# Splitting the 576 tokens of a unit into two halves of 288 in the token mixing of an attention-mixer kernel

## Chip, core and metric

The kernel runs on one core of one Trainium2 chip. The metric is device time in microseconds (us) of one execution, taken as the median of several runs of the same kernel.

## What is computed

For 8 batches and 8 heads, with 576 tokens and 64 channels per head, the reference does linear attention and then a two-stage mixer, all in float32:

```
q_s = softmax(q, over the 64 channels);  k_s = softmax(k, over the 576 tokens)
kv  = k_s^T v                 per head, 64 x 64
x   = q_s kv                  heads side by side: 576 tokens x 512 channels per batch
h   = relu(x^T w_tok1) w_tok2        576 -> 256 -> 576, mixes tokens
u   = x + h^T
out = u + relu(u w_ch1) w_ch2        512 -> 1536 -> 512, mixes channels
```

## The kernel before

**Units and groups.** A unit is a pair of heads of one batch, so it covers 128 channels and 576 tokens. There are 32 units (NU), four per batch. The rows of a unit are stored as five chunks of 128: four chunks hold the tokens 0 to 511, and the fifth holds the last 64 tokens (TL) twice. The eight batches of 576 tokens stand in one row of 4608 token columns, cut into nine groups (NG) of 512 columns. A batch therefore ends inside a group, at column `edge` of the batch, and every unit writes to two groups. The arrays `uT[g]` hold a group's u, split into a high and a low part ("uh" and "ul"), in which the matmuls of the channel mixing read it.

**Channel mixing.** It takes most of the time and is written out as a list of steps: `ch1(g, f)` (12 matmuls of 512 columns, line 488), its ReLU by ACT (L491) and the low part by DVE (L492), and one step later `ch2` (12 matmuls of 512 columns, L648). The last two groups are done in another way (lines 618 to 641, matmuls L597). The work of the units is put between these steps by hand (`put(at, ...)`, lines 803 to 842), and a scheduler of the framework that goes by a time simulation orders instructions where the program leaves it open.

**Early units.** The first 8 units (batches 0 and 1, "early") run before the channel mixing starts. The token weights are loaded and converted to float32 by DVE and ACT in the same stretch. `stage_qT` turns q with TensorE and copies it out (L341, L344). `stage_y` and `stage_h1` are matmuls L375 and L383. `stage_u` makes u in two pieces: a float32 matmul with `kvf` (L428, recorded as two passes) and six matmuls with the second token weight (`token_products`, L412), all of 320 columns in the first piece and of 256 in the second.

**Late units.** The other 24 units run `stage_us`. Here the 576 token columns are taken by the half of a 128-row chunk in which they lie ("side" 0 or 1): side 0 has five runs of 64 tokens, 320 columns, and side 1 has four, 256 columns. The token weights are read in those runs with a step (`cols`, lines 443 to 446). After the 12 `token_products` (six per side, L412) come four float32 matmuls of 64 x 64 (L458), one for each side and head; each is recorded as two passes. They lie on the four quarters of the array: the side gives the rows, the head gives the columns. Their moving operand is `stack`, which `stage_qT` fills from a DVE transpose (L352) in 16 pieces of 32 rows, 11 by DVE and 5 by ACT (L362). Then `empty` moves each bank to uh (ACT, L416) and ul (DVE, L417), in two pieces per side where the group's edge falls within the side; it writes every other run of 64 columns. Only the columns of one step stand in the code:

```
w = u["kvf"][rows, hs] if side == h else u["kvo"][rows]
to = t[hs, 0 : n * D].rearrange("p (c t) -> p c t", t=D)
nc.tensor.matmul(to, w, u["stack"][rows, h, 0:n, :], start=False, stop=True)
```

**The last 64 tokens twice.** In late units `softmax_q` splits q into a high part qh (ACT, L117) and a low part ql (POOL, L118). In the fifth chunk, rows 64 to 127 of qh are replaced by those of ql (L300, ACT, 64 rows), so that two matmuls do there what takes three in the other chunks. In early units the second copy is kept out by zeros in the upper half of `w1f` (L210, L214), and in k^T v by zeros in v and in its column of ones (L60).

**Loads.** `load_v` brings v in three transfers on SP's queue: two of the four whole chunks (L172, one per head, runs of 256 bytes) and one of 64 rows of the fifth (L173). The first loads go out in this order: kt and q of unit 0, three pieces of weights, v of unit 0, kt and q of unit 1, v of unit 1. One memory of eight banks serves all matmul results; two banks are held by a late unit's two sides.

Of the kernel before, what the change touches and what calls it, by code (L numbers as in the profile page):

```python
# [20 lines left out]
def attn_mixer_kernel(ctx: ExitStack, tc: tile.TileContext, q, k, kt, v, wt, out, dims):  # L21
# [9 lines left out]
    C1 = C + 1  # L31
    S0 = C * P
    TL = S - S0
    NG = B * S // CW
    NU = B * NJ
    NE = 2 * NJ
# [20 lines left out]

    def v_places(t):
        nc.gpsimd.memset(t[:, :, :, D : D + 1], 1.0)
        nc.gpsimd.memset(t[TL:P, C, :, :], 0.0)  # L60
        return t

    v_ring = [v_tile(const)]
# [2 lines left out]
    nc.gpsimd.memset(ones, 1.0)  # L66


    ebias = const.tile([P, 1], F32, name="ebias")
    nc.gpsimd.memset(ebias, -(896.0 + 20.0) * 2.0**23)  # L70

# [34 lines left out]
            cw[f] = [t[:, f - f0, :, x, :] for x in range(4)]  # L106

    ch_rows(0, F_HEAD)

    Q = 32  # L110

    def f32(ap):
        return ap.bitcast(F32)
# [54 lines left out]
    def load_v(n):  # L168
        if n < NU and n not in v_of:
            t = v_ring[n % 2 if n < NE or n >= PAIRED else 0]  # L170
            for h in range(2):
                nc.sync.dma_start(t[:, 0:C, h, 0:D], v[n][:, 0:C, h * D : (h + 1) * D])  # L172
            nc.sync.dma_start(t[0:TL, C, :, 0:D], v[n][0:TL, C, :].rearrange("p (h d) -> p h d", h=2))  # L173
            v_of[n] = t

    def load_weights(i, n=CW, out=None):
# [30 lines left out]
    def load_tok1():  # L207

        flat = w1f.rearrange("p c t -> p (c t)")
        nc.gpsimd.memset(w1f[TL:P, C, :], 0.0)  # L210
        for i in range(N1):
            load_weights(AT_T1 + i, out=flat[:, i * CW : (i + 1) * CW])
        load_weights(AT_TAIL, TOK, out=w1t)
        nc.scalar.copy(w1f[0:TL, C, :], w1t[0:TL])  # L214

    def split_tok1():
        split(w1h, w1l, w1f[:, 0:C, :], nc.vector)
# [55 lines left out]
    def softmax_q(u):  # L273
        G = 2 * C1
        st = sm.tile([P, 3, G], F32, name="st")
        qc = u["q"]
        qt = qc.rearrange("p c (h d) -> p (c h) d", h=2)
        nc.vector.tensor_reduce(st[:, 0, :], qt, axis=AX.X, op=ALU.max)
        if u["n"] < NJ or NE <= u["n"] < NE + NJ:

            nc.vector.tensor_scalar(st[:, 0, :], st[:, 0, :], -1.0, None, op0=ALU.mult)
            for i in range(G):
                one = slice(i, i + 1)
                nc.scalar.activation(
                    qt[:, i, :], qt[:, i, :], AF.Exp, bias=st[:, 0, one], accum_out=st[:, 1, one]
                )
# [12 lines left out]

        nc.scalar.copy(qh[TL:P, C, :], f32(ql[TL:P, C, :]))  # L300
        u["qh"], u["ql"] = qh, ql

    def stage_kv(u):
# [29 lines left out]
    def stage_qT(u):  # L333

        qx = u["q"]
        if u["early"]:
            qt = early.tile([P, S], F32, name="qt")
            t = ps_unit()
            for c in range(C):
                nc.tensor.transpose(t[:, c * P : (c + 1) * P], qx[:, c, :], f32(ident))  # L340
            nc.scalar.copy(qt[:, 0:S0], t)  # L341
            t = ps_unit()
            nc.tensor.transpose(t[:, 0:P], qx[:, C, :], f32(ident))
            nc.scalar.copy(qt[:, S0:S], t[:, 0:TL])  # L344
            u["qt"] = qt
            return

        stack = wk.tile([P, 2, S], F32, name="stack")[:, :, 0 : C1 * D]
        u["stack"] = stack = stack.rearrange("p h (c t) -> p h c t", t=D)

        turned = cv.tile([P, C1 * P], U32, name="cv_s").bitcast(F32).rearrange("p (c t) -> p c t", t=P)
        nc.vector.transpose(turned, qx)  # L352
        k = 0
        for x in range(P // Q):
            side, at = divmod(x * Q, D)
            for y in range(P // Q):
                h, row = divmod(y * Q, D)
                row += side * D
                eng = (nc.vector.tensor_copy, nc.vector.tensor_copy, nc.scalar.copy)[k % 3]
                k += 1  # L360
                n = C1 - side
                eng(stack[row : row + Q, h, 0:n, at : at + Q], turned[x * Q : (x + 1) * Q, 0:n, y * Q : (y + 1) * Q])  # L362

    def stage_y(u):
# [32 lines left out]

    emptied = []

    def token_products(u, t, N, cols, start, stop):  # L400
        mm = []
        for n in range(NT):
            mm += [
                (u["hh"][:, n, :], cols(w2h, n)),
                (u["hh"][:, n, :], cols(w2l, n)),
                (u["hl"][:, n, :], cols(w2h, n)),
            ]
        for i, (a, w) in enumerate(mm):
            to = t[:, 0:N]
            if len(w.shape) == 3:  # L410
                to = to.rearrange("p (c t) -> p c t", t=D)
            nc.tensor.matmul(to, a, w, start=start and i == 0, stop=stop and i == len(mm) - 1)  # L412

    def empty(uh, ul, src):
        emptied[:] = [
            nc.scalar.copy(uh, src).ins,  # L416
            nc.vector.tensor_tensor(ul, src, f32(uh), op=ALU.subtract).ins,  # L417
        ]

    def stage_u(u, half):  # L420
        b, j = u["b"], u["j"]
        edge = (b + 1) * CW - b * S
        cut = min(max(edge, S - 320), 320)
        n0, n1 = ((0, cut), (cut, S))[half]
        N = n1 - n0
        ns = slice(n0, n1)
        t = ps_unit()
        nc.tensor.matmul(t[:, 0:N], u["kvf"], u["qt"][:, ns], start=True, stop=False)  # L428
        token_products(u, t, N, lambda w, n: w[:, n, ns], False, True)
        for g, a0, a1 in ((b, n0, min(n1, edge)), (b + 1, max(n0, edge), n1)):  # L430
            if a0 < a1:
                at = b * S + a0 - g * CW
                uh, ul = (x[:, j, at : at + a1 - a0] for x in uT[g])
                empty(uh, ul, t[:, a0 - n0 : a1 - n0])

    def stage_us(u):
        b, j = u["b"], u["j"]
        edge = (b + 1) * CW - b * S  # L440
# [18 lines left out]
        for side, t in enumerate(banks):  # L459
            n = C1 - side  # L460
            src = t[:, 0 : n * D].rearrange("p (c t) -> p c t", t=D)
            m = len([c for c in range(n) if c * P + side * D < edge])
            for g, c0, c1 in ((b, 0, m), (b + 1, m, n)):
                if c0 < c1:
                    at = (b * S + c0 * P + side * D - g * CW) // D
                    uh, ul = (
                        x[:, j, :].rearrange("p (c t) -> p c t", t=D)[:, at : at + 2 * (c1 - c0) - 1 : 2, :] for x in uT[g]
                    )
                    empty(uh, ul, src[:, c0:c1, :])


    drained = []
# [434 lines left out]
    out_end(NG - 1, acc, True)  # L907


def pieces(w_tok1, w_tok2, w_ch1, w_ch2):  # L910

    import numpy as np

    S, TOK = w_tok1.shape
    C, TL, NT = S // P, S % P, TOK // P
# [3 lines left out]
    tail[0, :, :TOK] = np.concatenate([w_tok1[C * P :]] * 2)  # L919
# [44 lines left out]
```

## Time and profile before

| | |
|---|---|
| median of 3 runs | 797.1 us (796.87 to 797.65) |
| profiled execution | 798.31 us, of it a span of 796.5 us from its first to its last instruction |
| TensorE busy | 781.0 us of the span, 4478 matmul records |
| DVE, ACT, POOL busy | 526.9, 331.9 and 83.4 us |
| mean granted TensorE clock | 0.994 of full speed |
| moved by DMA | 65.10 MB, 64276 packets |

The profile is a recording of one execution on the chip. PE is TensorE (matmuls), PEld its weight loads, DVE is VectorE, ACT is ScalarE, POOL is GpSimd; SPq is SyncE's queue that issues transfers. L458 is line 458 of the kernel. A matmul's recorded duration reaches into the next one, since matmuls are pipelined, so the time that one costs is read from start to start. Of an f32 matmul the two passes are recorded one by one.

### The profile page before, as it was taken

Reading aid. Unit: us, or ns where it says so; the run is one execution under the profiler, and the core shown is the slowest. Engines: PE = TensorE matmul, PEld = TensorE weight load, DVE = VectorE, ACT = ScalarE, POOL = GpSimd, SP = SyncE. Lnnn points to the kernel's source line nnn. Section 1 sums busy time; section 2 is a strip of 40 time slices with the busy share of each in tenths; the row PEclk is TensorE's granted clock in tenths of the full one; section 3 lists DMA queues with packets and bytes.
Section 4 is the critical chain, followed back from the end, with each engine's and each line's share of the span. In section 5 each row is a group of like instructions: output and inputs, shape, how many; then the busy total and the mean of one; then the engine's idle time right before and its main releaser. Section 6 shows DMA issues by size and latency. Waiting matters only on the chain.

```text
span 796.5 us, 12193 instructions
## 1 busy us (share of the span) xinstructions
PE 781.0 (98%) x4478; PEld 651.9 (82%) x4478; DVE 526.9 (66%) x1224; ACT 331.9 (42%) x896; POOL 83.4 (10%) x72
## 2 busy tenths in 40 slices
PE   6899999999999999999999999999999999999997
PEld 5688888888888788888888888888888888888886
DVE  6889999876776445655575555563767458975440
ACT  6977554455643343243433434343434413332100
POOL 1000010011112111020200201111111000000020
PEclk8899999999999999999999999999999999999999
DMA  9754333324334221513132222212240000000011
GB/s 289 236 160 132 105 126 107 107 78 128 87 102 136 65 75 35 152 36 99 39 106 67 80 57 80 92 54 81 51 126 18 1 1 32 22 1 0 1 67 40
DMA packets 64276, 65.10 MB, mean 82 GB/s; under 512 B 41432, under 2 KB 44760, under 8 KB 64216
## 3 DMA queue, kind: packets, MB, share of 16 engines
q1 hardware_dynamic: 59608, 56.06, 23.9%
q10 hardware_dynamic: 4608, 8.26, 2.7%
q8 instruction: 35, 0.57, 0.3%
q14 instruction: 25, 0.20, 0.1%
HBM read 54.85 MB, written 9.45 MB: 81 GB/s over the span
## 4 chain that ended last, share of the span: by engine, by line
PE 94%; DVE 2%; DMA 1%; SPq 1%; ACT 1%; issue 0%; DVEq 0%
PE ps_o L648 33%; PE ps_h L488 29%; PE ps_h L597 7%; PE ps_h L375 6%; PE ps_h L412 6%; PE ps_h L648 4%; PE ps_h L310 2%; PE ps_h L458 2%; PE ps_h L383 2%; DMA kt_t<-in_kt 1%; PE ps_o L375 1%; PE ps_o L412 1%; PE ps_o L428 0%; DVE mc L241 0%; PE ps_h L428 0%; DVE stg L197 0%
## 5 line engine op out<-in xcount | busy, mean ns | idle before, releaser
L648 PE MATMUL ps_o<-h2h,cw 128*128 128x512 f32 x768 | 225.5, 391 | 0.0
L488 PE MATMUL ps_h<-uh,cw 128*128 128x512 f32 x672 | 210.1, 393 | 0.0
L648 PEld LDWEIGHTS ps_o<-h2h,cw 128*128 128x128 f32 x768 | 142.5, 188 | 29.8 <-DVE stg L685 0.5
L492 DVE SCALAR_TENSOR_TENSOR h2l<-ps_h,h2h 128x512 fp32r<-128x512 f32 x84 | 57.8, 689 | 152.6 <-ACT h2h L491 152.6
L488 PEld LDWEIGHTS ps_h<-uh,cw 128*128 128x128 f32 x672 | 123.7, 188 | 24.5 <-issue 0.5
L648 PE MATMUL ps_o<-h2l,cw 128*128 128x512 f32 x384 | 137.3, 391 | 0.0
L488 PE MATMUL ps_h<-ul,cw 128*128 128x512 f32 x336 | 131.0, 390 | 0.0
L648 PEld LDWEIGHTS ps_o<-h2l,cw 128*128 128x128 f32 x384 | 71.9, 188 | 15.3 <-DVE h2l L492 0.3
L118 POOL TENSOR_TENSOR ql<-q_t,qh 128x640 fp32r<-128x640 f32 x24 | 38.2, 1590 | 421.2 <-ACT qh L117 383.6
L491 ACT ACTIVATE h2h<-ps_h 128x512 fp32r<-128x512 f32 x84 | 50.0, 595 | 71.9 <-PE ps_h L488 70.8
L488 PEld LDWEIGHTS ps_h<-ul,cw 128*128 128x128 f32 x336 | 63.1, 188 | 13.4
L362 DVE COPY stack<-cv_s 32x160 f32<-32x160 f32 (+1 forms) x264 | 56.2, 231 | 3.6 <-PE ps_h L458 0.7
L270 POOL TENSOR_TENSOR k_t<-k_t,mb 128x640 f32<-128x640 f32 x24 | 38.2, 1590 | 119.4 <-DMA mb<-row 83.3
L271 ACT ACTIVATE k_t<-k_t 128x640 f32<-128x640 f32 x24 | 17.8, 741 | 72.1 <-POOL k_t L270 70.7
L506 DVE TENSOR_TENSOR ul<-ps_h,ul 128x512 f32<-128x512 f32 x40 | 27.5, 692 | 24.2 <-PE ps_h L597 23.9
L416 ACT CAST uh<-ps_h 128x128 fp32r<-128x128 f32 (+4 forms) x104 | 27.6, 288 | 30.7 <-PE ps_h L458 20.2
L362 ACT COPY stack<-cv_s 32x128 f32<-32x128 f32 (+1 forms) x120 | 36.9, 308 | 2.8 <-DVE cv_s L352 1.5
L417 DVE TENSOR_TENSOR ul<-ps_h,uh 128x128 fp32r<-128x128 f32 (+4 forms) x104 | 30.8, 312 | 6.0 <-ACT uh L416 5.1
L412 PE MATMUL ps_h<-w2h,hh 128*128 128x320 f32 (+1 forms) x112 | 33.7, 302 | 0.0
L412 PE MATMUL ps_h<-w2l,hh 128*128 128x320 f32 (+1 forms) x112 | 33.1, 298 | 0.0
L648 PE MATMUL ps_h<-cw 128*128 128x512 f32 x144 | 33.0, 389 | 0.0
L412 PE MATMUL ps_h<-w2h,hl 128*128 128x320 f32 (+1 forms) x112 | 32.6, 298 | 0.2 <-DVE hl L391 0.2
(249 smaller groups left out, 1283.8 us busy)
## 6 DMA issues: line engine op xcount, KB each, us to landing
stg<-in_w SPq DMA_DIRECT2D x28, 512.0 KB, 4.2
kt_t<-in_kt SPq DMA_DIRECT2D x32, 320.0 KB, 2.9
q_t<-in_q SPq DMA_DIRECT2D x32, 320.0 KB, 3.4
k_t<-in_k SPq DMA_DIRECT2D x24, 320.0 KB
out<-stg ACTq DMA_DIRECT2D x27, 256.0 KB, 2.0
v_t<-in_v SPq DMA_DIRECT2D x46, 128.0 KB, 2.7
part<-in_v SPq DMA_DIRECT2D x18, 128.0 KB, 2.5
mb<-row SPq DMA_DIRECT2D x23, 64.0 KB, 3.0
```

The lines of the kernel that those rows point to most:

```text
L118: return lo_eng.tensor_tensor(lo, src, f32(hi), op=ALU.subtract).ins
L270: nc.gpsimd.tensor_tensor(kx, kx, mb.unsqueeze(1).broadcast_to([P, C1, P]), op=ALU.subtract)
L362: eng(stack[row : row + Q, h, 0:n, at : at + Q], turned[x * Q : (x + 1) * Q, 0:n, y * Q : (y + 1) * Q])
L375: nc.tensor.matmul(y[:, 0:TOK], a, w, start=(i == 0), stop=(i == len(mm) - 1))
L412: nc.tensor.matmul(to, a, w, start=start and i == 0, stop=stop and i == len(mm) - 1)
L416: nc.scalar.copy(uh, src).ins,
L417: nc.vector.tensor_tensor(ul, src, f32(uh), op=ALU.subtract).ins,
L488: nc.tensor.matmul(t, cw[f][x][:, n, :], w, start=(i == 0), stop=(i == 3 * NJ - 1))
L491: nc.scalar.activation(hh, t, AF.Relu).ins,
L492: nc.vector.scalar_tensor_tensor(hl, t, 0.0, f32(hh), op0=ALU.max, op1=ALU.subtract).ins,
L597: nc.tensor.matmul(t, x(n), w[n], start=(n == 0 and i == 0), stop=(n == 1 and i == 2))
L648: nc.tensor.matmul(to, cw[f][x][:, n0 + n, :], w, start=(first and i == 0), stop=(last and i == 2))
```

## The change

The last 64 tokens (Q is now 32) are divided between the two halves of the rows: rows 0 to 31 of the fifth chunk hold tokens 512 to 543, rows 32 to 63 hold them again, rows 64 to 95 hold tokens 544 to 575 and rows 96 to 127 hold those again. Each half of the rows then has 4 x 64 + 32 = 288 tokens, and the token columns are ordered by halves, in the second token weight, in `uT` and in the output (the host puts the output's columns back and is not timed). `stage_u` and `stage_us` both work on two contiguous pieces of 288 columns; a batch's edge falls into one of the two pieces only. The rows of the second copy ("twins") are two blocks of 32. v comes in two transfers of five chunks, with its zeros from the host. The core of the diff (the host's reordering of weights and inputs is left out):

```diff
+    Q = TL // 2
+    W = S // 2
+    twins = [slice(x, x + Q) for x in (Q, 3 * Q)]
...
         nc.gpsimd.memset(t[:, :, :, D : D + 1], 1.0)
-        nc.gpsimd.memset(t[TL:P, C, :, :], 0.0)
+        for x in twins:
+            nc.gpsimd.memset(t[x, C, :, D : D + 1], 0.0)
...
+    once = const.tile([P, 1], F32, name="once")
+    nc.gpsimd.memset(once, 1.0)
+    for x in twins:
+        nc.gpsimd.memset(once[x], 0.0)
...
             for h in range(2):
-                nc.sync.dma_start(t[:, 0:C, h, 0:D], v[n][:, 0:C, h * D : (h + 1) * D])
-            nc.sync.dma_start(t[0:TL, C, :, 0:D], v[n][0:TL, C, :].rearrange("p (h d) -> p h d", h=2))
+                nc.sync.dma_start(t[:, :, h, 0:D], v[n][:, :, h * D : (h + 1) * D])
...
-        nc.scalar.copy(w1f[0:TL, C, :], w1t[0:TL])
+        nc.scalar.activation(w1f[:, C, :], w1t, AF.Copy, scale=once)
...
-        nc.scalar.copy(qh[TL:P, C, :], f32(ql[TL:P, C, :]))
+        for x in twins:
+            nc.scalar.copy(qh[x, C, :], f32(ql[x, C, :]))
...
-            nc.scalar.copy(qt[:, 0:S0], t)
+            sides = qt.rearrange("p (s x) -> p s x", s=2)
+            chunks = t.rearrange("p (c s t) -> p s c t", c=C, s=2)
+            nc.scalar.copy(sides[:, :, 0 : S0 // 2].rearrange("p s (c t) -> p s c t", c=C), chunks)
...
-            nc.scalar.copy(qt[:, S0:S], t[:, 0:TL])
+            nc.scalar.copy(sides[:, :, S0 // 2 :], t[:, 0:P].rearrange("p (s t) -> p s t", s=2)[:, :, 0:Q])
...
-        stack = wk.tile([P, 2, S], F32, name="stack")[:, :, 0 : C1 * D]
-        u["stack"] = stack = stack.rearrange("p h (c t) -> p h c t", t=D)
+        stack = wk.tile([P, 2, S], F32, name="stack")
+        u["stack"] = stack[:, :, 0:W]
+        stack = stack[:, :, 0 : C1 * D].rearrange("p h (c t) -> p h c t", t=D)
...
-                n = C1 - side
+                n = C1 if at == 0 else C
...
-    def token_products(u, t, N, cols, start, stop):
+    def token_products(u, t, half, start, stop):
+        ns = slice(half * W, (half + 1) * W)
         mm = []
         for n in range(NT):
             mm += [
-                (u["hh"][:, n, :], cols(w2h, n)),
-                (u["hh"][:, n, :], cols(w2l, n)),
-                (u["hl"][:, n, :], cols(w2h, n)),
+                (u["hh"][:, n, :], w2h[:, n, ns]),
+                (u["hh"][:, n, :], w2l[:, n, ns]),
+                (u["hl"][:, n, :], w2h[:, n, ns]),
             ]
         for i, (a, w) in enumerate(mm):
-            to = t[:, 0:N]
-            if len(w.shape) == 3:
-                to = to.rearrange("p (c t) -> p c t", t=D)
-            nc.tensor.matmul(to, a, w, start=start and i == 0, stop=stop and i == len(mm) - 1)
...
+            nc.tensor.matmul(t[:, 0:W], a, w, start=start and i == 0, stop=stop and i == len(mm) - 1)
+
+    def empty(u, t, half):
...
-        cut = min(max(edge, S - 320), 320)
-        n0, n1 = ((0, cut), (cut, S))[half]
-        N = n1 - n0
-        ns = slice(n0, n1)
-        t = ps_unit()
-        nc.tensor.matmul(t[:, 0:N], u["kvf"], u["qt"][:, ns], start=True, stop=False)
-        token_products(u, t, N, lambda w, n: w[:, n, ns], False, True)
...
+    def stage_u(u, half):
+        t = ps_unit()
+        nc.tensor.matmul(t[:, 0:W], u["kvf"], u["qt"][:, half * W : (half + 1) * W], start=True, stop=False)
+        token_products(u, t, half, False, True)
+        empty(u, t, half)
...
     def stage_us(u):
...
         banks = []
-        for side in range(2):
-            def cols(w, n):
-                t = w[:, n, side * D :]
-                t = w[:, n, :].rearrange("p (x t) -> p x t", t=D)
-                return t[:, side : 2 * C + 1 : 2, :]
...
+        for half in range(2):
             t = ps_unit()
-            token_products(u, t, (C1 - side) * D, cols, True, False)
+            token_products(u, t, half, True, False)
             banks.append(t)
-        for side, t in enumerate(banks):
-            rows = slice(side * D, (side + 1) * D)
-            n = C1 - side
+        for half, t in enumerate(banks):
+            rows = slice(half * D, (half + 1) * D)
             for h in range(2):
                 hs = slice(h * D, (h + 1) * D)
-                w = u["kvf"][rows, hs] if side == h else u["kvo"][rows]
-                to = t[hs, 0 : n * D].rearrange("p (c t) -> p c t", t=D)
-                nc.tensor.matmul(to, w, u["stack"][rows, h, 0:n, :], start=False, stop=True)
...
+                w = u["kvf"][rows, hs] if half == h else u["kvo"][rows]
+                nc.tensor.matmul(t[hs, 0:W], w, u["stack"][rows, h, :], start=False, stop=True)
+        for half, t in enumerate(banks):
+            empty(u, t, half)
```

## Rows read from the trace of the kernel before

**Rows 1.** The page, busy time of the engines and the chain that ended last.

```profile
PE 781.0 (98%) x4478; PEld 651.9 (82%) x4478; DVE 526.9 (66%) x1224; ACT 331.9 (42%) x896; POOL 83.4 (10%) x72
...
PE 94%; DVE 2%; DMA 1%; SPq 1%; ACT 1%; issue 0%; DVEq 0%
```

**Rows 2.** Busy time by stretches: us, busy of each engine, PEclk, DMA share, GB/s.

```profile
10.00:20.00 10.00, 5.32 (x37) 4.18 (x37) 9.20 (x23) 6.67 (x26) 0.00 (x0) 0.76 1.07 335
20.00:30.00 10.00, 7.43 (x51) 5.29 (x50) 9.21 (x26) 9.96 (x38) 0.00 (x0) 0.90 0.83 258
30.00:40.00 10.00, 9.05 (x61) 7.96 (x62) 8.75 (x24) 8.93 (x35) 0.00 (x0) 0.83 0.64 217
400.00:660.00 260.00, 260.00 (x1571) 217.38 (x1570) 158.66 (x400) 101.47 (x265) 32.62 (x21) 1.00 0.21 62
```

**Rows 3.** TensorE in order of time, one late unit: start, us, line, shape.

```profile
401.08 0.31 PE L412 MATMUL ps_h<-w2h,hh 128*128 128x320 f32 x1
...
401.97 0.28 PE L412 MATMUL ps_h<-w2h,hh 128*128 128x256 f32 x1
...
402.77 0.48 PE L458 MATMUL ps_h<-stack,part 64*64 64x320 f32 x1
402.78 0.48 PE L458 MATMUL ps_h<-stack,kvo 64*64 64x320 f32 x2
...
403.05 0.38 PE L458 MATMUL ps_h<-stack,kvo 64*64 64x256 f32 x1
...
403.10 0.43 PE L458 MATMUL ps_h<-stack,kvo 64*64 64x320 f32 x1
403.46 0.80 PE L310 MATMUL ps_h<-v_t,k_t 128*64 128x65 f32 x20
```

**Rows 4.** Groups by form, the 64 x 64 matmuls with `kvo`: busy us, mean ns.

```profile
L458 PE MATMUL ps_h<-stack,kvo 64*64 64x320 f32 x48 | 18.0, 454 | 0.0
...
L458 PE MATMUL ps_h<-stack,kvo 64*64 64x256 f32 x48 | 15.4, 402 | 0.0
```

**Rows 5.** The chain of waits in the early units, four pieces: start, us, what.

```profile
69.17 0.54 PE ps_o L428 x2
...
70.15 0.43 PE ps_h L428 x2
...
75.17 0.59 PE ps_o L412 x4
75.76 0.47 PE ps_h L412 x4
```

**Rows 6.** Groups by form, ACT: busy us, mean ns | idle before, releaser.

```profile
L320 ACT ACTIVATE kvf<-ps_h,rs 64x64 f32<-64x64 f32 x34 | 10.6, 311 | 29.3 <-DVE rs L316 28.9
...
L416 ACT CAST uh<-ps_h 128x128 fp32r<-128x128 f32 x36 | 9.2, 266 | 13.2 <-PE ps_h L458 7.3 <-DVE ul L417 5.8
...
L300 ACT CAST qh<-ql 64x128 fp32r<-64x128 f32 x24 | 7.2, 298 | 33.5 <-POOL ql L118 23.7 <-DVE stg L685 9.7
...
L416 ACT CAST uh<-ps_h 128x64 fp32r<-128x64 f32 x22 | 4.5, 216 | 12.5 <-PE ps_h L458 10.8 <-DVE ul L417 1.4
```

**Rows 7.** TensorE's waits: us in total, times, longest.

```profile
PE ps_h L375 <- ACT w1f L214: 0.9, 1, 0.9
```

**Rows 8.** SP's queue in the head, in order of time: start, us.

```profile
3.06 1.93 SPq L172 DMA_DIRECT2D v_t<-in_v  x2
...
5.03 1.53 SPq L173 DMA_DIRECT2D v_t<-in_v  x1
```

**Rows 9.** The chain of waits in the head, the second kt.

```profile
6.61 5.86 DMA kt_t<-in_kt
```

**Rows 10.** Busy time by stretches in the head, columns as in Rows 2.

```profile
4.00:5.00 1.00, 0.99 (x5) 0.69 (x4) 0.97 (x3) 0.18 (x1) 0.00 (x0) 1.00 0.71 187
5.00:6.00 1.00, 0.30 (x3) 0.30 (x4) 0.68 (x2) 0.90 (x2) 0.00 (x0) 1.00 0.89 242
6.00:7.00 1.00, 1.00 (x12) 1.00 (x11) 0.00 (x0) 1.00 (x7) 0.00 (x0) 1.00 0.76 311
```

More of the change, by code (lines that the diff above doesn't have):

```diff
@@ L108, in attn_mixer_kernel @@
     ch_rows(0, F_HEAD)
-    Q = 32
     def f32(ap):
@@ L209, in load_tok1 @@
         flat = w1f.rearrange("p c t -> p (c t)")
-        nc.gpsimd.memset(w1f[TL:P, C, :], 0.0)
         for i in range(N1):
@@ L403, in token_products @@
             mm += [
-                (u["hh"][:, n, :], cols(w2h, n)),
-                (u["hh"][:, n, :], cols(w2l, n)),
-                (u["hl"][:, n, :], cols(w2h, n)),
+                (u["hh"][:, n, :], w2h[:, n, ns]),
+                (u["hh"][:, n, :], w2l[:, n, ns]),
+                (u["hl"][:, n, :], w2h[:, n, ns]),
             ]
         for i, (a, w) in enumerate(mm):
-            to = t[:, 0:N]
-            if len(w.shape) == 3:
-                to = to.rearrange("p (c t) -> p c t", t=D)
-            nc.tensor.matmul(to, a, w, start=start and i == 0, stop=stop and i == len(mm) - 1)
[L414 to L420, printed above, removed]
+            nc.tensor.matmul(t[:, 0:W], a, w, start=start and i == 0, stop=stop and i == len(mm) - 1)
+    def empty(u, t, half):
         b, j = u["b"], u["j"]
         edge = (b + 1) * CW - b * S
-        cut = min(max(edge, S - 320), 320)
-        n0, n1 = ((0, cut), (cut, S))[half]
-        N = n1 - n0
-        ns = slice(n0, n1)
-        t = ps_unit()
-        nc.tensor.matmul(t[:, 0:N], u["kvf"], u["qt"][:, ns], start=True, stop=False)
-        token_products(u, t, N, lambda w, n: w[:, n, ns], False, True)
+        n0, n1 = half * W, (half + 1) * W
         for g, a0, a1 in ((b, n0, min(n1, edge)), (b + 1, max(n0, edge), n1)):
@@ L433, in stage_u @@
                 uh, ul = (x[:, j, at : at + a1 - a0] for x in uT[g])
-                empty(uh, ul, t[:, a0 - n0 : a1 - n0])
+                src = t[:, a0 - n0 : a1 - n0]
+                emptied[:] = [
+                    nc.scalar.copy(uh, src).ins,
+                    nc.vector.tensor_tensor(ul, src, f32(uh), op=ALU.subtract).ins,
+                ]
+    def stage_u(u, half):
[3 more added lines that the diff above has]
+        empty(u, t, half)
@@ L438, in stage_us @@
     def stage_us(u):
-        b, j = u["b"], u["j"]
-        edge = (b + 1) * CW - b * S
         banks = []
-        for side in range(2):
-            def cols(w, n):
-                t = w[:, n, side * D :]
-                t = w[:, n, :].rearrange("p (x t) -> p x t", t=D)
-                return t[:, side : 2 * C + 1 : 2, :]
+        for half in range(2):
             t = ps_unit()
-            token_products(u, t, (C1 - side) * D, cols, True, False)
+            token_products(u, t, half, True, False)
@@ L459, in stage_us @@
[L459 to L469, printed above, removed]
+                w = u["kvf"][rows, hs] if half == h else u["kvo"][rows]
@@ L907, in attn_mixer_kernel, with rows_and_columns @@
     out_end(NG - 1, acc, True)
+def rows_and_columns(S):
+    import numpy as np
+    C, TL = S // P, S % P
+    Q = TL // 2
+    whole, tail = np.arange(C * P).reshape(C, 2, P // 2), np.arange(C * P, S).reshape(2, Q)
+    rows = np.concatenate([whole.ravel(), np.repeat(tail[:, None], 2, axis=1).ravel()])
+    columns = np.concatenate([np.concatenate([whole[:, x].ravel(), tail[x]]) for x in range(2)])
+    return rows, columns
 def pieces(w_tok1, w_tok2, w_ch1, w_ch2):
@@ L914, in pieces @@
     S, TOK = w_tok1.shape
+    w_tok2 = w_tok2[:, rows_and_columns(S)[1]]
     C, TL, NT = S // P, S % P, TOK // P
@@ L918, in pieces @@
     tail = np.zeros((2, P, CW), w_tok1.dtype)
-    tail[0, :, :TOK] = np.concatenate([w_tok1[C * P :]] * 2)
+    tail[0, :, :TOK] = w_tok1[rows_and_columns(S)[0][C * P :]]
     tail[1, :, : NT * TL] = w_tok2[:, C * P :].reshape(NT, P, TL).transpose(1, 0, 2).reshape(P, NT * TL)
@@ L935 @@
     c, tl, nu = s // P, s % P, b * h // 2
-    twice = np.concatenate([np.arange(s), np.arange(s - tl, s)])
+    twice, columns = rows_and_columns(s)
+    once = np.ones((P, c + 1, 1), inputs["v"].dtype)
+    once[:, c].reshape(4, -1)[1::2] = 0
     def rows(x):
@@ L947 @@
         "in_kt": np.ascontiguousarray(inputs["k"].reshape(nu, 2, s, d)[:, :, twice].transpose(0, 1, 3, 2)).reshape(nu, P, -1),
-        "in_v": rows(inputs["v"]),
+        "in_v": np.where(once > 0, rows(inputs["v"]), np.float32(0)),
         "in_w": np.ascontiguousarray(pieces(*weights)),
@@ L962 @@
     o = r.results[0]["out_0"]
-    return np.ascontiguousarray(o.transpose(0, 3, 1, 2)).reshape(b, s, dm)
+    o = o.transpose(0, 3, 1, 2).reshape(b, s, dm)
+    return np.ascontiguousarray(o[:, np.argsort(columns)])
```

## The prediction

> **What bounds the kernel now.** The page comes first: TensorE is busy for 781.0 of 796.5 us, and 94% of the chain that ended last is TensorE's own work [rows 1]. So nearly every microsecond that TensorE's stream of instructions loses or gains is one of the kernel. The stretches say where this does not hold. From 400 to 660 us TensorE is busy for 260.00 of 260 us, while ACT has 101.47 us of work and DVE 158.66 [rows 2]; there only TensorE's own cost counts. From 10 to 30 us TensorE does 5.32 and 7.43 us of work in each 10, DMA is full in the first of the two (share 1.07) and ACT in the second (9.96 of 10), and the granted clock averages 0.76, 0.90 and then 0.83 in the 10 us after [rows 2]; there loads, conversion and clock set the pace. So I read two things in detail: the token stage of one late unit in order of time, and the first 13 us.
>
> **The four quarters of the array, the main term.** In a late unit the 12 `token_products` start at 401.08, the four float32 matmuls of 64 x 64 at 402.77, and the next instruction, of the full height of the array, at 403.46 [rows 3]. The block takes 0.69 us. Its first passes all start within 0.02 us (402.77 and 402.78), so the four quarters work at the same time. Side 1 (256 columns) starts a second pass at 403.05, side 0 (320 columns) its last at 403.10 [rows 3]: each quarter goes at its own pace, the longer side ends the block, and the shorter one's quarters stand idle at its end. With 288 columns on either side the longest pass has 32 columns fewer. The price of a column is in the groups by form: a pass of 320 columns takes 454 ns, one of 256 takes 402 [rows 4]; 52 ns for 64 columns, so 26 ns a pass and 52 ns for the two of a quarter. The group has 48 records of each size, two passes for each of 24 units [rows 4]: 24 x 52 ns = **-1.25 us**.
>
> The bounds are these. If the whole block scaled with its columns, 0.69 x 32/320 = 0.069 us, or -1.65 us. If four quarters at once are slower than two, the pace to take is that of the first pass of side 1, which had all four at work: 256 columns from 402.78 to 403.05, 1.05 ns a column. Side 1 then ends near 403.32 (402.78 and twice 0.27); the longer side would need 402.78 + 640 x 0.81 = 403.30 at the slope's pace and at this one 403.45, so the rows allow either. With four at 1.05 ns a column and two at 0.81, the block now is 512 columns in 0.54 us and the last 128 in 0.10, and after the change 576 in 0.605: -0.036 us a block, or -0.9 us. I take the slope, since it compares the two lengths directly.
>
> The Trainium skill's page "TensorE: Matmul & The Clock Gate" (part 3, measured speedup) speaks for the smaller end: four row tiles at once gave 3.07 times, not four times, the speed of one, so that quarters which now run alone at the end of a block would lose their advantage. By an estimate from that page, with the pace of four a quarter below that of one, the gain would be about 0.9 us. The start times above hold no such slowdown for certain, so the rule stays a bound.
>
> **Token products, nothing.** The columns stay 576 per product, cut otherwise. Six of 320 columns take 401.08 to 401.97, 0.148 us each; six of 256 take until 402.77, 0.80 us with the change to the quarters in it [rows 3]. In the early units, where the operand is contiguous, 320 columns take 0.59/4 = 0.148 and 256 take 0.47/4 = 0.118 us [rows 5]: the runs of 64 of the late units cost nothing now, so contiguous ones bring nothing. A linear price puts 288 at 0.133, twice that is 0.266, the old sum. If 288 cost as much as 256 or as 320 it would be 0.03 us less or more for each of the 6 x 32 pairs, but no row shows a step. The early f32 product follows the same line: 0.54 and 0.43 us for two passes of 320 and 256 columns [rows 5], twice 0.485 after.
>
> **ACT and DVE, hidden.** A late unit's u is emptied in four pieces before (three in batch 7) and in three after: 92 pieces become 72, on both engines, with the same columns. On ACT, 64 columns take 216 ns and 128 take 266 [rows 6], so a piece costs 166 ns beside its columns, and 20 fewer save 3.3 us on ACT and about as much on DVE. Against that, L300 (298 ns, [rows 6]) becomes two copies of 32 rows; rows of a tile work side by side, so I count each at the full 298: 24 x 0.298 = 7.2 us more on ACT. Its cover is the idle time of ACT, 158 us of the 260 after 400 us [rows 2]. The pieces of `stack` keep their number and columns; two of the 160 wide ones only go to other engines. The first half of an early unit now also waits for the copy of the fifth chunk (L344), which stands right behind L341 on ACT and well ahead of the product. The added memsets lie on an idle POOL in the first microseconds. None of this is on TensorE's path; if the cover is gone, see the rivals.
>
> **The tail of w1f, at most 0.1 us.** L214 becomes a copy with a scale of each row, over 128 rows. TensorE waits 0.9 us for it once [rows 7], so it is on the path. A scaled copy of 64 columns takes 311 ns (L320), a plain one 216 [rows 6]: +0.1 us at most, 0 at least; I take **+0.05**.
>
> **Loads of v in the head.** In the head SP issues v of unit 0 as two transfers in 1.93 us from 3.06 and a third in 1.53 us from 5.03 [rows 8], and only then, at 6.61, the second kt; DVE and all that follows wait for that load, 5.86 us [rows 9]. After, the third issue is gone, so kt leaves up to 1.5 us earlier. That helps only as far as the DMA engines had nothing to do: their share was 0.71, 0.89 and 0.76 from 4 to 7 us [rows 10], against 1.07 when full [rows 2], 0.85 us of work missing at most. The other way, v grows from 288 to 320 KB: 32 KB at 187 GB/s [rows 10] is 0.17 us a unit and 0.35 for the two v loads of the head. Between -0.85 and +0.35 I take **-0.1**, nearer the upper end, because an issue that takes 1.5 us is one that is held up by a queue with work in it. Late loads are asked for a unit ahead with a DMA share of 0.21 [rows 2] and cost nothing.
>
> **The sum.** -1.25 + 0.05 - 0.1 = -1.3 us. The profiled execution took 798.31 us, of which 1.8 lie outside its span, and would take 797.0; it stands 1.2 us above the median, so the median goes from 797.1 to **795.8 us**. Its own range, from the bounds, is -1.65 - 0.85 = 794.6 to -0.9 + 0.1 + 0.35 = 796.7.
>
> **Rivals.** *The block does not shrink.* If the quarters share a feed, the total of columns sets the block, which stays the same, and only the small terms are left: 797.1. For it speaks that the pace of the first pass (1.05 ns a column) is above the slope's 0.81; against it, that the shorter side runs ahead.
>
> *The clock gives back more.* A granted clock of 0.83 over the 10 us from 30 [rows 2] is 3.4 us at 1.2 GHz, the rest at 2.4; before it, from 20 to 30 us, TensorE had stood idle for 2.6 us. If an earlier kt closes that gap enough to keep the clock up, 1.7 us of TensorE's work come back: 797.1 - 1.3 - 1.7 = 794.1. The same stretch can come once more in the head, if the larger v makes the gap longer: 797.1 - 1.3 + 1.7 + 0.35 = 797.9.
>
> *Slower.* The second copy of L300 stands on ACT ahead of the next ReLU (L491), whose result TensorE wants one step later. If that ReLU were late, 0.3 us would be lost per unit, 24 x 0.298 - 1.3 = +5.9: 803.0. It decides where ACT reaches the ReLU after its matmuls have ended by more than the step that covers it, 12 matmuls of 512 columns. L300 already waits for POOL, 23.7 us in all [rows 6], without a wait of TensorE's; that speaks against it.
>
> **How the numbers follow.** About 0.2%, 1.6 us, is what a measurement of this kernel can tell from no change, so the line to faster lies at 795.5, just below the forecast. Chances: forecast 0.55, no shrinking 0.16, clock gained 0.17, clock lost 0.06, slower 0.06. Faster is the clock's 0.17 and about a third of the forecast's 0.55, 0.37 in all; slower is 0.06; the same is the rest, 0.57. The range takes in the forecast's own, the unchanged block and the edge of the gained clock: 794.2 to 797.6.
>
> **What would show it.** Right: both passes of the 64 x 64 matmuls near 428 ns, the block at 0.63 to 0.64 us in each of 24 units, the products at 0.133 us, 72 late pieces, no new wait of TensorE. Wrong: a block of 0.69 us; products at another price than 0.133; a wait for h2h or qh on TensorE; another length of the stretches at the lower clock in the first 40 us, which alone could outweigh the main term.

## The result: 805.56 us, slower where no change was forecast

The changed kernel takes 805.56 us in the median of 6 runs, the kernel before 797.19: a ratio of 1.0107 [1.0097, 1.0118]. The forecast was 795.8 within 794.2 to 797.6, and the 8.4 us that came instead belong to none of its rivals. The profiled execution has a span of 803.3 us against 796.5.

The page after, busy time and the chain that ended last, and TensorE's group by form for the 64 x 64 matmuls with `kvo`:

```profile
PE 779.0 (97%) x4478; PEld 651.0 (81%) x4478; DVE 523.5 (65%) x1204; ACT 338.0 (42%) x900; POOL 84.1 (10%) x77
...
PE 80%; DVE 9%; DMA 5%; ACT 3%; issue 1%; POOL 1%; SPq 1%; DVEq 0%; ACTq 0%; POOLq 0%
```

```profile
L454 PE MATMUL ps_h<-stack,kvo 64*64 64x288 f32 x96 | 16.9, 428 | 0.0
```

TensorE is busy for 2.0 us less than before [rows 1], and each pass takes the 428 ns that were forecast. But the chain, 94% TensorE before [rows 1], is 80% now, and DVE, DMA and ACT have 17% of it. (These shares are not the loss: from a single wait the chain runs back over tens of microseconds of the other engines' work.) So the question is not what TensorE does, but what it waits for. Its waits after (engine, line and releaser; us in total, times, longest):

```profile
PE ps_h L317 <- ACT k_t L277: 4.3, 1, 4.3
...
PE ps_h L317 <- DVE h2l L479: 1.9, 1, 1.9
...
PE ps_h L385 <- ACT w1f L220: 1.1, 1, 1.1
PE ps_o L635 <- ACT h2h L478: 1.0, 1, 1.0
```

The 4.3 us and the 1.0 us have no line in the list of before; the wait for h2l was 0.64 us there. TensorE in order of time shows where the largest stands and what follows it (start, us, what, idle before):

```profile
186.84 0.39 PE L635 MATMUL ps_o<-h2l,cw 128*128 128x512 f32 x1
191.56 1.12 PE L317 MATMUL ps_h<-v_t,k_t 128*64 128x65 f32 x20 [4.33 <-ACT k_t L277]
192.61 0.58 PE L385 MATMUL ps_h<-w1h,qh 128*128 128x256 f32 x1
192.99 0.41 PE L385 MATMUL ps_h<-w1l,qh 128*128 128x256 f32 x1
193.21 0.41 PE L385 MATMUL ps_h<-w1h,ql 128*128 128x256 f32 x1
...
195.32 0.29 PE L385 MATMUL ps_h<-w1th,qh 128*128 128x256 f32 x1
195.44 0.28 PE L385 MATMUL ps_h<-w1tl,qh 128*128 128x256 f32 x1
```

After the idle 4.33 us the matmuls of 256 columns start 0.21 us apart (192.99 to 193.21), where the last two stand 0.12 apart. The stretch beside it says why (columns as in rows 2):

```profile
192.00:195.00 3.00, 3.00 (x25) 2.88 (x22) 1.84 (x6) 2.37 (x13) 0.00 (x0) 0.50 0.24 55
```

The granted clock is 0.50 from 192 to 195 us, that is 1.2 GHz in place of 2.4; half of 3 us, 1.5 us, is lost on top of the wait. So 1.00 + 4.33 + 1.5 and the 1.2 us by which the wait for h2l grew (it ends at 282 us; why it grew was not followed) make 8.0 us. Up to 150 us nothing is lost: the same step of `ch1` starts there in both, first before, then after:

```profile
150.42 0.62 PE L488 MATMUL ps_h<-uh,cw 128*128 128x512 f32 x2
```

```profile
150.27 0.61 PE L475 MATMUL ps_h<-uh,cw 128*128 128x512 f32 x2
```

The seventh late unit's 64 x 64 block starts 7.9 us later than before (303.17 against 295.28); from there on 1.1 us is gained, which leaves the 6.8 us between the spans. (The profiled execution before stood 1.2 us above its median.)

**What made k_t late.** The chain of waits, followed back from 191.56 us (start, us, what):

```profile
149.19 4.48 DMA stg<-in_w
...
158.84 3.26 DMA stg<-in_w
...
166.78 0.69 DVE cw L126
167.47 0.75 DVE cv_s L362
...
175.91 2.44 ACT q_t L290 x14
...
178.55 0.59 DVE stg L671
...
181.94 0.60 DVE stg L672
182.53 0.73 DVE q_t L299
...
184.60 0.72 DVE st L284
...
187.37 0.77 ACT q_t L290 x4
...
190.88 0.63 ACT k_t L277
...
191.56 1.12 PE ps_h L317 x20
```

In the kernel before the same view, from 149.91 to 192 us, holds TensorE's rows alone, matmul after matmul. Here it starts at the load of a channel weight (in_w), goes through VectorE's conversion of it (L199 to L206, the last low part by L126 at 166.78), the token work queued behind it, and then through the output of group 1 (`out_end`, L671 and L672), which stands ahead of the normalisation of q of unit 9 ("q norm", L299). Before, the q norm came first and `out_end` after it:

```profile
173.97 0.82 DVE L293 TENSOR_TENSOR q_t<-q_t,st 128x640 f32<-128x640 f32 x1
...
176.38 2.47 DVE L684 TENSOR_TENSOR stg<-ps_o,uh 128x512 f32<-128x512 f32 x4
```

VectorE in order of time, the low parts of the last weight tiles (last columns: shape, count), first in the kernel before, then after:

```profile
133.59 0.68 DVE L118 TENSOR_TENSOR cw<-cv_s,cw 128x512 fp32r<-128x512 f32 x1
135.72 0.68 DVE L118 TENSOR_TENSOR cw<-cv_s,cw 128x512 fp32r<-128x512 f32 x1
141.06 0.69 DVE L118 TENSOR_TENSOR cw<-cv_s,cw 128x512 fp32r<-128x512 f32 x1
...
162.32 0.69 DVE L118 TENSOR_TENSOR cw<-cv_s,cw 128x512 fp32r<-128x512 f32 x1
```

```profile
130.19 1.46 DVE L126 TENSOR_TENSOR cw<-cv_s,cw 128x512 fp32r<-128x512 f32 x2
140.20 1.46 DVE L126 TENSOR_TENSOR cw<-cv_s,cw 128x512 fp32r<-128x512 f32 x2
...
159.50 1.29 DVE L126 TENSOR_TENSOR cw<-cv_s,cw 128x512 fp32r<-128x512 f32 x2
166.78 0.69 DVE L126 TENSOR_TENSOR cw<-cv_s,cw 128x512 fp32r<-128x512 f32 x1 [0.69 <-ACT cw L125]
```

Before, a tile ends every few microseconds; after, two end close together and then none for some 8 us. The program's order of VectorE's instructions says the same; a to e are the five steps of a conversion (L192 to L199 before, L199 to L206 after), the number is the tile, L the low part:

```
before  a24 L b24 c24 d24 a25 e24 b25 c25 L d25 e25 a26 L b26 c26 a27 d26
after   a23 a24 b23 c23 b24 d23 c24 e23 d24 e24 L L a25 b25 a26 c25 b26
```

For these tiles only two staging tiles are there (`more_pools` is closed at F_MORE). Taken in step, both come free together, both loads start together, and VectorE has nothing to convert until they land. Its waits for these loads, in the whole run, first before, then after:

```profile
DVE cv_s L192 <- DMA stg<-in_w: 6.2, 7, 2.5
```

```profile
DVE cv_s L199 <- DMA stg<-in_w: 9.6, 7, 2.9
```

From the first to the last of the last eight low parts it is 28.7 us before (133.59 to 162.32) and 35.8 after (the second of the pair at 130.19 starts at 130.97, the last at 166.78).

So the theory is that the order of VectorE's instructions, which the scheduler chose anew, costs the 8 us, and not the halves themselves.

### The profile page after: what moved, and what is told of

Same layout as the page of the kernel before. It is cut to its first block, busy times and chain, and to the rows that moved or that the text cites. A ratio compares the mean times of both kernels' runs of the same rounds, so it can differ in the third digit from the quotient of the medians.

```text
span 803.3 us, 12112 instructions
## 1 busy us (share of the span) xinstructions
PE 779.0 (97%) x4478; PEld 651.0 (81%) x4478; DVE 523.5 (65%) x1204; ACT 338.0 (42%) x900; POOL 84.1 (10%) x77
## 4 chain that ended last, share of the span: by engine, by line
PE 80%; DVE 9%; DMA 5%; ACT 3%; issue 1%; POOL 1%; SPq 1%; DVEq 0%; ACTq 0%; POOLq 0%
PE ps_o L635 27%; PE ps_h L475 23%; PE ps_h L584 7%; PE ps_h L385 6%; PE ps_h L420 5%; PE ps_h L635 4%; DMA stg<-in_w 2%; PE ps_h L317 2%; PE ps_h L454 2%; PE ps_h L393 1%; DVE stg L204 1%; ACT q_t L290 1%; DMA kt_t<-in_kt 1%; DVE cv_s L206 1%; DMA mb<-row 1%
## 5 line engine op out<-in xcount | busy, mean ns | idle before, releaser
L126 POOL TENSOR_TENSOR ql<-q_t,qh 128x640 fp32r<-128x640 f32 x24 | 38.6, 1607 | 422.3 <-ACT qh L125 271.7
L372 DVE COPY stack<-cv_s 32x128 f32<-32x128 f32 (+1 forms) x264 | 55.7, 229 | 5.1 <-PE ps_h L454 2.2
L277 ACT ACTIVATE k_t<-k_t 128x640 f32<-128x640 f32 x24 | 17.7, 738 | 64.0 <-POOL k_t L276 64.0
L372 ACT COPY stack<-cv_s 32x160 f32<-32x160 f32 (+1 forms) x120 | 37.4, 311 | 2.3 <-DVE cv_s L362 1.0
L432 ACT CAST uh<-ps_h 128x288 fp32r<-128x288 f32 (+8 forms) x84 | 25.3, 318 | 26.0 <-PE ps_h L454 19.8
L420 PE MATMUL ps_h<-w2h,hh 128*128 128x288 f32 x112 | 33.5, 300 | 0.0
L420 PE MATMUL ps_h<-w2l,hh 128*128 128x288 f32 x112 | 33.1, 297 | 0.0
L433 DVE TENSOR_TENSOR ul<-ps_h,uh 128x288 fp32r<-128x288 f32 (+8 forms) x84 | 29.2, 349 | 5.5 <-ACT uh L432 4.6
L420 PE MATMUL ps_h<-w2h,hl 128*128 128x288 f32 x112 | 32.6, 296 | 0.0
```

Source lines behind the costliest of these rows:

```text
L126: return lo_eng.tensor_tensor(lo, src, f32(hi), op=ALU.subtract).ins
L420: nc.tensor.matmul(t[:, 0:W], a, w, start=start and i == 0, stop=stop and i == len(mm) - 1)
```

## The experiments

The kernel before was run again beside each group: 797.44 us with the first four, 796.93 with the next four, 796.57 with the last two. Narrow form of the theory at first: `out_end` ahead of the q norm is the cause.

**1. Early pieces alone.** The kernel before with an early unit's tokens cut at 288 instead of 320.

```diff
-        cut = min(max(edge, S - 320), 320)
+        cut = S // 2
```

> Kernel before, with the early units' pieces of 288 and 288 columns in place of 320 and 256, nothing else. Theory 1 (order): the new piece lengths make the scheduler order DVE's instructions so that the output of group 1 goes ahead of the normalisation of q of the second late unit, which makes that unit's k^T v late; then this kernel is slow as well, 801 to 806 us, with a wait of TensorE of 3 to 5 us for k_t near 187 us. Theory 2 (a real cost of the late units' new halves, the second q copy or the larger v): those are all as before here, so 797 us and no such wait.

796.77 us, 0.9994 [0.9985, 1.0003]. The scheduler did turn the order round, as VectorE's rows show (first `out_end`, then q norm), but the wait that this leaves is small (third row, TensorE):

```profile
171.78 1.37 DVE L684 TENSOR_TENSOR stg<-ps_o,uh 128x512 f32<-128x512 f32 x2 [1.86 <-PE ps_o L648]
...
178.46 0.82 DVE L293 TENSOR_TENSOR q_t<-q_t,st 128x640 f32<-128x640 f32 x1
```

```profile
185.26 0.80 PE L310 MATMUL ps_h<-v_t,k_t 128*64 128x65 f32 x20 [0.29 <-ACT k_t L271]
```

The narrow form falls: the inversion alone costs 0.3 us of waiting. The low parts were spread out here (29.8 us for the last eight).

**2. All but the early pieces.** The changed kernel with early units cut at 320 again.

```diff
...
     def stage_u(u, half):
...
-        token_products(u, t, half, False, True)
-        empty(u, t, half)
+        n0, n1 = ((0, 320), (320, S))[half]
...
+        token_products(u, t, n0, n1, False, True)
+        empty(u, t, n0, n1)
...
```

> Changed kernel, with the early units' pieces back at 320 and 256 columns, everything else as changed. Theory 1 (order): the output of group 1 stands behind the normalisation again, the wait for k_t near 187 us is gone, and what is left is the gain of the late blocks: 795 to 796.5 us. Theory 2 (cost of the late halves, the second q copy or the larger v): all of that is still there, so 803 to 806 us.

796.70 us, 0.9997 [0.9982, 1.0012]. All the rest of the change is in this kernel, the twins, the v loads and the quarters of 288, and the 8 us are gone; the time is 0.2 us above theory 1's range. VectorE's order is nearly that of before, 28.6 us for the last eight tiles, and TensorE's list of waits has no k_t L277.

**3. The order of the drain, mended.** The changed kernel with `out_end` of group 1 ordered behind the q norm.

```diff
...
-                out_end(*pend[:2], i != F_HEAD)
+                with behind(normed if pend[0] == 1 else []):
+                    out_end(*pend[:2], i != F_HEAD)
```

> Changed kernel, with one more rule of order: DVE issues the output of group 1 only behind the normalisation of q that precedes it in the program. Theory 1 in its narrow form (this one inversion is the cost): the waits of 1.0 and 4.3 us and the stretch at the lower clock behind them go, 798 to 800 us are left. Rival: the inversion is a symptom, the conversion of the channel weights on DVE is some 4 us late in any case and unit 9 is late with it; then the gain is below 2 us, 803 to 805 us.

801.47 us, 1.0058 [1.0040, 1.0077]. The time lies between the two theories. The k_t wait is gone, and half of the loss; the tiles still go in pairs (36.1 us), the q norm is still late (178.13), and TensorE waits elsewhere:

```profile
PE ps_h L318 <- DVE h2l L480: 1.5, 1, 1.5
PE ps_h L421 <- ACT hh L401: 1.4, 1, 1.4
...
PE ps_h L394 <- ACT kvf L328: 0.7, 1, 0.7
```

**4. The v loads alone.** The kernel before with v in two transfers, zeroed twins included.

```diff
...
-                nc.sync.dma_start(t[:, 0:C, h, 0:D], v[n][:, 0:C, h * D : (h + 1) * D])
-            nc.sync.dma_start(t[0:TL, C, :, 0:D], v[n][0:TL, C, :].rearrange("p (h d) -> p h d", h=2))
+                nc.sync.dma_start(t[:, :, h, 0:D], v[n][:, :, h * D : (h + 1) * D])
...
```

> Kernel before, with v in two transfers of five chunks in place of three, nothing else. Theory 1 (order): the inversion is not there, so 796.5 to 798 us. Theory 2 in the form that the loads are the cost (32 KB more per unit, fewer issues in the head): 799 to 803 us, with the loss in the first 45 us.

798.61 us, 1.0028 [1.0016, 1.0040]: 1.2 us slower, and between the two theories. A wait for k_t of 0.94 us at 41.56 us is new, but the profiled execution's first late block starts no later for it (179.50, before 179.68), so it does not explain the loss. Whether that is the load or once more the order, run 10 takes up.

**5. The pairs, taken apart.** The changed kernel, where a tile's conversion starts only behind the masking step of the tile before.

```diff
...
-            t = load_weights(at + f).rearrange("p (n m) -> p n m", n=NJ)
+            with behind(masked if f >= F_MORE else []):
+                t = load_weights(at + f).rearrange("p (n m) -> p n m", n=NJ)
...
```

> The changed kernel, whole, with one rule on the order of instructions: from the ninth weight tile on, VectorE begins a tile's conversion only behind the masking step of the tile before (L202). In the order written, that takes apart the pairs in which the changed kernel steps through two tiles at once, and puts the q norm (L299) back ahead of the draining of the last weight gradients. Theory A (the pairs expose the load of the two staging tiles, the last conversion ends some 4 us late, and the wait of 4.33 us for k_t at 187 us follows from it): last conversion ends by 164 us, no wait over 1 us near 187, 796 to 798. Rival B (the lateness comes from further up, the first 100 us, and the pairs only show it): conversion still ends at 166 or later, 801 to 804.

(The "weight gradients" are the output of group 1: this kernel has no gradients.)

797.71 us, 1.0014 [1.0000, 1.0028], as theory A has it. One rule of order gives back over 7 us, with all of the change in place; it takes the pairs apart and moves `out_end` behind the q norm at once, so it does not price the two separately. One expectation missed: the last low part stands at 165.12, not before 164, since the first pair stayed and the rule costs VectorE time as well (33.1 us for the last eight). With the q norm in front again (175.88), this lateness costs 0.84 us of waiting.

**6. The pairs, made in the kernel before.** Its last eight weight tiles are converted two at a time in step, nothing else.

```diff
...
+        each_of(lambda n, w0, w1, s: nc.vector.tensor_scalar(s, w1, 20, 0x7FF, op0=ALU.logical_shift_right, op1=ALU.bitwise_and))
+        each_of(mask)
...
-                load_ch(load_at[i])
+                (load_two if load_at[i] >= F_MORE else load_ch)(load_at[i])
```

> The kernel before, with its quarters and its loads as they are, but its last eight weight tiles converted by VectorE two at a time in step, as the changed kernel does by itself. Theory A (the pairs are the cause): the conversion ends at 166 us or later against 163, TensorE waits for k_t near 187 us by 2 to 5 us, 800 to 805. Rival B (the pairs are harmless, something in the early stretch is late): 796 to 798, no such wait.

801.92 us, 1.0069 [1.0049, 1.0089]. TensorE's waits:

```profile
PE ps_h L520 <- DVE cw L118: 2.3, 2, 1.3
PE ps_h L342 <- ACT k_t L303: 2.2, 1, 2.2
```

The k_t wait comes, at 187.22 us as in the changed kernel, and `out_end` goes ahead of the q norm by itself. Two things were not expected: the last conversion ends at 165.5 us and not at 166 or later, and TensorE also waits twice for the weights as such (0.96 and 1.30 us), which it doesn't in the changed kernel. The three waits make 4.5 of the 5.0 us.

**7. Another load of v in the changed kernel**, to change the order from elsewhere: the shared group of both heads in a third transfer.

```diff
-                nc.sync.dma_start(t[:, :, h, 0:D], v[n][:, :, h * D : (h + 1) * D])
+                nc.sync.dma_start(t[:, 0:C, h, 0:D], v[n][:, 0:C, h * D : (h + 1) * D])
+            nc.sync.dma_start(t[:, C, :, 0:D], v[n][:, C, :].rearrange("p (h d) -> p h d", h=2))
```

> The changed kernel with the load of v in three transfers instead of two: the four whole groups of each head separately, and the shared group of both heads in one. It computes the same with the same twins; what changes is the early loads and, through them, the order of VectorE's instructions, in which the last weight tiles are no longer taken in pairs. Theory A (order decides, not what the halves cost): 795.5 to 797.5, no wait over 1 us near 187. Rival C (the halves themselves cost some 8 us, whatever the order): 803 to 807.

797.71 us, 1.0012 [1.0001, 1.0022], 0.2 us above theory A's range and far from rival C's. The last eight take 28.6 us, and no wait stands between 67 and 252 us. One transfer more for v, and with it another order, moves the kernel by over 7 us.

**8. The second copy of q alone.** The prediction's slower rival.

```diff
-        nc.scalar.copy(qh[TL:P, C, :], f32(ql[TL:P, C, :]))
+        for x in (TL, TL + 32):
+            nc.scalar.copy(qh[x : x + 32, C, :], f32(ql[x : x + 32, C, :]))
```

> The kernel before with the copy of the second half of the last 64 tokens (L300) made as two copies of 32 partitions each: one more ScalarE instruction in each of the calls, as the changed kernel has. Theory A (ScalarE has the room, nothing of the copies shows): 796.5 to 798. The rival of the prediction (the second copy delays the ReLU on ScalarE, TensorE waits for it in every step): 800 to 803, with waits of TensorE for hh from 400 us on.

798.29 us, 1.0022 [1.0010, 1.0034], between the two. No matmul of TensorE waits after 272 us, but in three of the 17 stretches from the seventh late block to the 24th its weight loads do, since h2h and h2l are stationary operands of `ch2`. TensorE's weight loads in the worst of the three:

```profile
437.49 0.30 PEld L649 LDWEIGHTS ps_o<-h2h,cw 128*128 128x128 f32 x2 [0.35 <-ACT h2h L492]
438.21 0.19 PEld L649 LDWEIGHTS ps_o<-h2l,cw 128*128 128x128 f32 x1 [0.43 <-DVE h2l L493]
```

These three stretches take 21.22, 21.42 and 21.23 us where others of their kind take 20.93, 1.1 us in all; the kernel before has one such (21.12). In all of them ACT makes the high part of q (L117) just ahead of the ReLU, and the ReLU comes late. So something like the prediction's rival is there, three times and behind another copy than the second one; in the profiled execution this makes 0.9 of the 1.4 us, and why there are three instead of one is not settled.

**9 and 10. Is there a gain once the order is kept?** Run 2's kernel timed once more, and the same with v in three transfers.

> The changed kernel with the first units cut at 320 and 256 columns again (the late units keep their 288 columns a half), timed once more and longer. VectorE's conversion steps then stand in nearly the order of the kernel before. Theory A (what the halves bring is the prediction's 1.3 us, and the order took it): 795.3 to 796.3 where the kernel before has 797, a ratio of 0.998 to 0.999. Rival D (the 1.25 us in the quarters are lost again in other small waits): a ratio of 1.000 or above.

> The same with v loaded in three transfers (the four whole groups of each head, and the shared group of both heads in one), as a candidate for a version faster than both. By the run of the kernel before with v in two transfers, which was 1.2 us slower, theory A gives another 0.5 to 1 us: 794.5 to 795.5, ratio 0.997 to 0.998. Rival (the price of v in two transfers was the order of that kernel, not the load): as the other one of this call, within 0.5 us.

796.64 us, 1.0001 [0.9989, 1.0012], and 796.83 us, 0.9998 [0.9988, 1.0007]. Neither is faster than the kernel before, so theory A's 1.3 us do not come through, and run 9's ratio is rival D's. The number of v transfers makes no difference here: the 1.2 us of run 4 aren't the load's price in this kernel. No version beats both; run 2's beats the changed kernel by 9 us.

**The runs side by side.** The middle columns are the two parts of the order, the fourth the waits of TensorE's matmuls between 150 and 195 us:

| kernel | last eight low parts, us | first on VectorE near 175 us | waits, us | ratio |
|---|---|---|---|---|
| before | 28.7 | q norm | none | 1 |
| 2 early pieces of 320 | 28.6 | q norm | none | 0.9997 |
| 7 v in three | 28.6 | q norm | none | 1.0012 |
| 9, 10 run 2 again, and with v in three | 28.9, 28.7 | q norm | none | 1.0001, 0.9998 |
| 4 v in two in before | 29.2 | q norm | none | 1.0028 |
| 8 two copies of q in before | 28.8 | q norm | none | 1.0022 |
| 1 early pieces alone | 29.8 | `out_end` | 0.3 | 0.9994 |
| 5 pairs taken apart | 33.1 | q norm | 0.8 | 1.0014 |
| 6 pairs in before | 31.6 | `out_end` | 4.5 | 1.0069 |
| 3 drain mended | 36.1 | q norm | 2.6 | 1.0058 |
| changed | 35.8 | `out_end` | 5.3 | 1.0107 |

The output in front alone costs little (run 1); late tiles alone cost half of the loss, in other waits (run 3); with both, k_t is 4 us late. Runs 5 and 6 show the cause from both sides, run 6 in direction and not in full: 5.0 of the 8.4 us, 2.3 of them in waits for the weights. Runs 4 and 8 have the order of before in both columns and are 1.2 and 1.4 us slow, so the two decide the large losses and not every one of a microsecond.

## Why the prediction was wrong

**The step that failed is one that it doesn't have.** It counted every instruction and let each keep its place; "ACT and DVE, hidden" sums their work and calls none of it TensorE's path. The description of the kernel had a scheduler that goes by a time simulation; the prediction put the order at nothing without saying so, and so without asking what hides it. The runs show 6.8 us there in its place, 5.3 of waiting between 178 and 192 us and 1.5 at the lower clock behind it, and 1.2 more in the later wait for h2l. In run 1, 32 columns moved from one early piece to another reordered VectorE some 100 us later; in runs 2 and 7 other details set the order back. That simulated times of the early pieces tip it is inferred from this, not shown. A rival would have been there to write: the conversion of the last weight tiles with two staging tiles, whose slack the trace could have bounded.

**The quarters: right mechanism, size 0.95 instead of 1.25 us.** From the first 64 x 64 matmul to the next instruction, the 24 blocks take 16.44 us together before and 15.49 after, 0.685 and 0.645 each. TensorE in order of time, one block of run 9, the first of the products ahead of it, and what follows:

```profile
402.32 0.29 PE L420 MATMUL ps_h<-w2h,hh 128*128 128x288 f32 x1
...
404.01 0.45 PE L454 MATMUL ps_h<-stack,part 64*64 64x288 f32 x1
404.02 0.46 PE L454 MATMUL ps_h<-stack,kvo 64*64 64x288 f32 x2
404.03 0.68 PE L454 MATMUL ps_h<-stack,part 64*64 64x288 f32 x2
404.31 0.41 PE L454 MATMUL ps_h<-stack,kvo 64*64 64x288 f32 x2
404.33 0.40 PE L454 MATMUL ps_h<-stack,part 64*64 64x288 f32 x1
404.66 0.80 PE L317 MATMUL ps_h<-v_t,k_t 128*64 128x65 f32 x20
```

It takes 0.65 us, from 404.01 to 404.66, as in the changed kernel, with both passes at the forecast 428 ns; but the second passes start 0.29 us after the first, for 288 columns 1.01 ns each. That is close to the pace of four at once (1.05 ns) that gave the prediction's lower bound, 0.9 us, and not the slope that it took: recorded durations shrank as forecast, and the time from start to start, which is what counts, by less. The estimate of about 0.9 us from the Trainium skill's page "TensorE: Matmul & The Clock Gate" (part 3, measured speedup) was right in size: by that rule, the trace agrees, with 0.95. The page's figure is for four row tiles and not for quarters like these. The rival that the block doesn't shrink is out.

**About half of that gain arrives, and the runs can't see it.** From the start of the seventh block on, no matmul waits for over 0.2 us in any of them, and the elapsed times are these, in us:

```
                    7th block starts   to the 24th   to the end
before                        295.28        353.74       147.48
changed                       303.17        353.16       146.97
run 2                         293.88        353.17       146.95
run 9 (same kernel)           296.63        353.17       146.90
```

From the seventh block to the 24th all seven executions with halves of 288 take 353.16 or 353.17 us, the five with the old quarters 353.71 to 354.61. Of the 0.6 us against the kernel before, 0.2 is its one late weight load (run 8 above). The other 0.4 is less than 17 blocks of 0.04, because in every second stretch from block to block both kernels take 20.93 us (in the first of these the `ch2` step behind the block takes 2.77 us in place of 2.72). Of the 0.5 us behind the 24th block, 0.2 is gained by the last change of step on TensorE (107.97 us after the block before, 107.76 after), and run 1, with the old quarters, takes 147.07 to the end as well. So of the 1.1 us, 0.4 can be put down to the quarters, and the rest is not shown to be theirs. Ahead of the seventh block one and the same kernel differs by 2.75 us between two profiled executions (293.88, 296.63), and the whole gain is under what the prediction called measurable.

**Token products** at nothing: right. Twelve of 288 columns take 1.69 us with the change to the quarters, as six of 320 and six of 256 did [rows 3]: 402.32 to 404.01 above.

**ACT and DVE**, hidden: right as far as it counts work. Late pieces fell to 72, DVE's work by 3.4 us; ACT's grew by 6.1 instead of 7.2 - 3.3 = 3.9, because the fewer pieces of uh saved it only some 1.7 us. As work this is unseen by TensorE; what was not hidden is the order of it. The copies of 32 rows cost a full copy each, as taken:

```profile
L307 ACT CAST qh<-ql 32x128 fp32r<-32x128 f32 x48 | 14.2, 297 | 23.7 <-POOL ql L126 23.3
```

**w1f and v**: the copy grew from 422 to 528 ns, as its bound has it. TensorE's wait for it went from 0.9 [rows 7] to 1.1 us; in run 1, with the old copy, it was 0.2, so more than the copy sets it. For v, the second kt left earlier as forecast (5.40 in place of 6.61) but took 7.51 us in place of 5.86, so VectorE began on it 0.4 us later (12.93 in place of 12.49), just past the bound of +0.35; in run 4, with the same two transfers, it began at 11.88. So -0.1 is neither shown nor refuted.

**The clock** moved in both places. From 30 to 40 us the granted clock was 1.00 after, 0.83 before [rows 2], as the rival has it; but the two executions of run 2's kernel show 0.83 and 1.00 there, so the change alone does not set it, and TensorE's matmuls waited 13.4 us up to 50 us in place of 10.1. At 150 us nothing of either is left. What counted were the 1.5 us after a wait that the prediction didn't see.

## What to carry to other kernels

Where a scheduler orders what the program leaves open, an edit has a term of its own: the order of every engine with slack. Compare the two orders before costing the edit, and look where a pool has just two buffers, since steps taken in pairs there free both at once and expose the load. A small gain in the bound engine is best read as elapsed time over a stretch without waits, of its matmuls and of its weight loads; and a one-line rule on the order (run 5) tells in one run whether an unexpected loss is the edit's or the schedule's.

## What the hardware showed unexpectedly

The wait of 4.33 us in mid-kernel was followed by 3 us at a granted clock of 0.50, which adds a third to its price; after the 2.25 us in run 6 the granted clock stayed at 1.00. And the list of TensorE's waits does not hold all of them: from the seventh block to the 24th, run 8 took 354.61 us and run 1 354.36 against 353.74 before, with the same late matmuls and no matmul that waits. The loss is in the lines of the weight loads (PEld), which wait for h2l or h2h up to 0.43 us, while the matmul before is still recorded as busy: three steps in run 8, two in run 1, one before, and none of this kind in the kernels with halves of 288.
